# Attention and two expert layers in one kernel: the planner counts more columns per matmul, and all remainders go to VectorE

## The chip, the cores and the metric

One core of a Trainium2 chip runs the whole program. The metric is the device time of one execution in microseconds. The engines are named as in the profile: PE (TensorE matmul), PEld (its weight load), DVE (VectorE), ACT (ScalarE), POOL (GpSimd), SP (SyncE, here the queue that issues most transfers).

## What is computed

The reference chains three layers; the part that matters here is the second and third.

```
x = attention(q, k, v, f)                      # 2304 tokens of 512 numbers
e = argmax of the router's logits per token    # 8 experts
x[e == i] = gate * (relu(x[e == i] @ w1[i]) @ w2[i])      # w1: 512x1024, w2: 1024x512
x = maximum(maximum(x @ m1, x @ m2), x @ m3) @ m_out      # 512x768 three times, 768x512
```

All is float32. Each product is made of three matmuls of split operands: the high part of a number is a rounded copy, the low part ("remainder") is the number minus that copy; high times high, high times low and low times high are summed (`mm3`, L905 to L908).

## The kernel before, in words

Attention runs first (to about 216 us of the span), then the tokens are sorted by expert, and `moe` (from L911) computes both expert layers. Its order is not written out by hand: every step is a task with an engine (or a choice of two), a cost in microseconds, a priority (a due time `now`), dependences, and a slot of a buffer pool that it takes or frees. `Sched.run` (L184) picks, again and again, the task that can start first by its own count of time, and among those that can start at the same moment the one with the smallest priority; it then issues that task's instructions. So the costs and due times fix the order of the instructions in each engine's queue; at run time each engine works its queue strictly in that order and semaphores do the waiting.

The expert stage loops over k = 0 to 7, the experts in order of size, with room for C = 384, 352, ... 256 tokens (`CAP`). For each:

- `ph` (L906 to L908): 8 hidden tiles f, 12 matmuls each of C columns, from the tokens `x0`, `x1` (high, low) and the weight pieces `w_1_k_q`, q = 0 to 3;
- `h` (L1135 on ACT, L1141 on DVE): relu, high part and remainder of a hidden tile;
- `py`: 16 steps (q, d) of 6 matmuls, from `h` and `w_2_k_q`, then a copy into Y;
- `expert_piece` (L955): a weight piece is loaded into one of 3 `stg` buffers (L964), its high part is copied (L934, mostly ACT) into one of 4 `ring` buffers, and its remainder is taken (L951), on DVE or POOL;
- `tokens` (L1054): three gathers of the next expert's tokens by POOL (`gat`, L1065, 3 buffers), each transposed on PE (`xt`, L1072) into one of the two `ps_o` PSUM buffers, and split there by ACT (L934) and DVE (L1083) into `x0`, `x1`. So `xt1_0`, `xt1_1`, `xt1_2` are the three transposes that expert 1's first `ph` needs, and `xt2_0` the first of expert 2.

Two side jobs run beside this. `side_work` (L880) computes gates and the table of output rows; its last part, `scatter_table` (L834), makes four rounds on DVE (`pi`, `rm`, `rq`, `ohp`, `cc`, `rr`: L841 to L853) that feed four rounds of five small matmuls `ctps` on PE (L859), and then copies the sum out (`T`, L863). `ctps` holds one of the same two `ps_o` buffers from the first round to that copy. Its priority is a fixed 30. `shared_piece` (L988) loads the third layer's weights, two halves a piece through one `std` buffer, decodes each half in five DVE operations (L1005 to L1020, tiles `dec` and `sd`), copies the high part (ACT) and takes the remainder `m` (L1030, DVE or POOL).

The third layer then runs in six chunks of 384 tokens: 18 products `pm` of 12 matmuls, maxima on DVE (`tm`, L1240), high part and remainder `g` (L1251), and three output products `po` (L1266 to L1268). The tokens of a chunk are split from Y by L1199.

Priorities come from these lines (the cost of a matmul group in `now` is its columns over 2400):

```
gap = 24 * C / 2400
...
xdone[k + 1] = tokens(k + 1, now + 4 * gap, h_pe, [sorted_])
```

and in `tokens` the transposes get the priority `use - 6`.

Of the kernel before, what the change touches and what calls it, by code (L numbers as in the profile page):

```python
# [37 lines left out]
MC = 384  # L38
# [872 lines left out]
def moe(tc, g, x_dram, w1, w2, m2, mo, out, rp, es):  # L911
# [15 lines left out]
    sd.bias = {"DVE": 1.0, "Pool": 0.3}  # L927
    act = lambda n: 0.06 + n / 1200
    dve = lambda n: 0.15 + n / 960
    ENG = {"ACT": nc.scalar, "DVE": nc.vector, "Pool": nc.gpsimd}  # L930

    def copy(e, out, in_):
# [17 lines left out]
    def low(e, w, t):  # L950
        ENG[e].tensor_tensor(out=w[:, 1], in0=t, in1=w[:, 0].bitcast(F32), op=ALU.subtract)  # L951

    weight, wsplit, ahead = {}, {}, {}

    def expert_piece(n, k, q, use, deps=(), eng="SP"):  # L955
        src = (w1, w2)[n - 1]
        key = n, k, q
        raw = {}

        def load(e):  # L960
            dq = nc.sync if eng == "SP" else nc.scalar
            t = raw[0] = stg.tile([128, 1024], F32, tag="stg", name=f"stg_{n}_{k}_{q}")
            r = reg(dq, "expi" if k else "expi0", k, E - 1)
            dq.dma_start(out=t, in_=src[bass.ds(r, 1), q].rearrange("o p c -> (o p) c"))  # L964

        def hi(e):
            weight[key] = ring.tile([128, 2, 1024], F32R, tag="ring", name=f"w_{n}_{k}_{q}")
            high(e, weight[key], raw[0])

        ld = sd.task(eng, 1.5 if eng == "SP" else 0.1, load, use - 8, list(deps) + [ahead.get("stg")], get=("stg", key), lat=2.0 if eng == "SP" else 3.5)  # L970
        th = sd.task(("ACT", "DVE"), (0.95, 0.67), hi, use - 3, [ld, ahead.get("ring")], get=("ring", key))
        ahead["stg"], ahead["ring"] = ld, th
        tl = sd.task(("DVE", "Pool"), (1.13, 2.3), lambda e: low(e, weight[key], raw[0]), use - 3, [th], rel=[("stg", key)])
        wsplit[key] = tl
        return ld, th

    def bits(raw, q, v, n):
        r = raw.rearrange("p (n w) -> p n w", w=2)[:, 256 * q:256 * q + 256]
        lo, hi = r[:, :, 0], r[:, :, 1]
        t = scr.tile([128, 256], I32, tag="dect", name=f"dt{n}", bufs=1)  # L980
        u = scr.tile([128, 256], I32, tag="decu", name=f"du{n}", bufs=1)
        nc.vector.tensor_scalar(out=t, in0=hi, scalar1=3, scalar2=0x3FFFFFF8, op0=ALU.logical_shift_left, op1=ALU.bitwise_and)
        nc.vector.tensor_scalar(out=u, in0=hi, scalar1=0x7FFFFFFF, scalar2=None, op0=ALU.bitwise_and)
        nc.vector.scalar_tensor_tensor(out=t, in0=hi, scalar=-0x40000000, in1=t, op0=ALU.bitwise_and, op1=ALU.bitwise_or)
        nc.vector.scalar_tensor_tensor(out=t, in0=lo, scalar=29, in1=t, op0=ALU.logical_shift_right, op1=ALU.bitwise_or)
        nc.vector.scalar_tensor_tensor(out=v, in0=u, scalar=float(897 << 20), in1=t.bitcast(F32), op0=ALU.is_ge, op1=ALU.mult)

    def shared_piece(key, early, use, deps):  # L988
        w, j = key
# [3 lines left out]
        for h in range(2):  # L993
# [48 lines left out]
                         get=("ring", key) if new else None)  # L1042
            if new:
                ahead["ring"] = th
            lows.append(sd.task(("DVE", "Pool"), (dve(512), 1.3), lo, use - 3, [th], rel=[(pool_, (key, h))]))
        wsplit[key] = lows
        return lows[-1]

# [55 lines left out]

    zero = [sd.task("ACT", 1.8, lambda e, d=d: clear(e, d), now + 16, [wsplit[1, 0, 3]]) for d in range(KC)]
    mkeys = [(w, j) for j in range(3) for w in range(3)] + [("o", j) for j in range(3)]
    total = now + sum(CAP) * 192 / 2400
    shared = [wsplit[1, 0, 3]]
    for i, key in enumerate(mkeys[:M2EARLY]):
        shared.append(shared_piece(key, True, now + 30 + (total - now - 34) * (i + 1) / M2EARLY, [shared[max(0, i - 1)]]))  # L1110
# [2 lines left out]
    hlast, yev_last = [], []  # L1113
    for k in range(E):
        C = CAP[k]
        gap = 24 * C / 2400
        h_lo, h_pe, base = [], [], now
        for f in range(FC):
            q = f // 2
            t0 = now  # L1120
            key = 1, k, q

            def hmm(e, f=f, q=q, k=k, C=C):
                w = weight[1, k, q].rearrange("p s (k f) -> p s k f", k=KC)
                ph = hh["p", k, f] = ps_h.tile([128, 512], F32, tag="y", name=f"ph{k}_{f}")
                fs = slice(128 * (f % 2), 128 * (f % 2) + 128)
                for kc in range(KC):
                    mm3(nc, ph[:, 0:C], w[:, 0, kc, fs], w[:, 1, kc, fs], X[k][0][:, kc, 0:C], X[k][1][:, kc, 0:C],
                        kc == 0, kc == KC - 1)

            def relu(e, f=f, k=k, C=C):
                ht = hh[k, f] = hp.tile([128, 2, PADW], F32R, tag=f"h{f}", name=f"h{k}_{f}")
                ph = hh["p", k, f]
                if e == "ACT":
                    nc.scalar.activation(out=ht[:, 0, 0:C], in_=ph[:, 0:C], func=AF.Relu)  # L1135
                else:
                    nc.vector.tensor_scalar(out=ht[:, 0, 0:C], in0=ph[:, 0:C], scalar1=0.0, scalar2=None, op0=ALU.max)

            def rest(e, f=f, k=k, C=C):
                ht, ph = hh[k, f], hh["p", k, f]  # L1140
                nc.vector.scalar_tensor_tensor(out=ht[:, 1, 0:C], in0=ph[:, 0:C], scalar=0.0,  # L1141
                                               in1=ht[:, 0, 0:C].bitcast(F32), op0=ALU.max, op1=ALU.subtract)

            pe_ = sd.task("PE", 12 * C / 2400, hmm, t0, [wsplit[key]] + xdone[k] + yall, get=("y", ("h", k, f)),
                          rel=[("ring", key)] if f % 2 else [])
            now += 12 * C / 2400
            rl = sd.task(("ACT", "DVE"), (act(C), dve(C)), relu, now + 1, [pe_] + yprev[q])
            h_lo.append(sd.task("DVE", dve(C), rest, now + 1, [rl], rel=[("y", ("h", k, f))]))
            h_pe.append(pe_)
        for q in range(4):  # L1150
            expert_piece(2, k, q, now + q * gap, [sorted_] if k else [])
        if k + 1 < E:
            for q in range(4):
                expert_piece(1, k + 1, q, now + 4 * gap + q * 24 * CAP[k + 1] / 2400, [sorted_])
            xdone[k + 1] = tokens(k + 1, now + 4 * gap, h_pe, [sorted_])
        order = [(q, d) for q in range(4) for d in range(KC)] if k + 1 < E else [(q, d) for d in range(KC) for q in range(4)]
        last, pieces = {}, {q: [] for q in range(4)}
        for i, (q, d) in enumerate(order):
            def ymm(e, q=q, d=d, k=k, C=C):
                if q == 0:  # L1160
                    hh["y", k, d] = ps_y.tile([128, 512], F32, tag="y", name=f"py{k}_{d}")
                py = hh["y", k, d]
                w = weight[2, k, q].rearrange("p s (f d) -> p s f d", f=2)
                for f in range(2):
                    fc = 2 * q + f
                    ds_ = slice(128 * d, 128 * d + 128)
                    mm3(nc, py[:, 0:C], w[:, 0, f, ds_], w[:, 1, f, ds_], hh[k, fc][:, 0, 0:C], hh[k, fc][:, 1, 0:C],
                        fc == 0, fc == FC - 1)

            end = not any(q2 == q for q2, _ in order[i + 1:])  # L1170
            last[d] = sd.task("PE", 6 * C / 2400, ymm, now, [wsplit[2, k, q], h_lo[2 * q], h_lo[2 * q + 1], last.get(d)],
                              get=("y", ("y", k, d)) if q == 0 else None, rel=[("ring", (2, k, q))] if end else [])
            pieces[q].append(last[d])
            now += 6 * C / 2400
            if q == 3:
                def yev(e, d=d, k=k, C=C):
                    o = Y[d][:, bass.ds(reg(ENG[e], "offi", k, YW - C), C)] if k else Y[d][:, 0:C]
                    copy(e, o, hh["y", k, d][:, 0:C])

                prev = [ydone[-1][d], zero[d]] if ydone else []  # L1180
                t = sd.task(("ACT", "DVE"), (act(C), dve(C)), yev, now, [last[d]] + prev + [sorted_], rel=[("y", ("y", k, d))])
                yev_last.append(t)
# [7 lines left out]
    def ysplit(c, use, before):  # L1190
        done = []
        for kc in range(KC):
# [7 lines left out]
                                     in1=X["y", c][0][:, kc, :].bitcast(F32), op=ALU.subtract)  # L1200

            th = sd.task(("ACT", "DVE"), (act(MC), dve(MC) / 2), hi, use - 4, [ydone[-1][kc]] + before)
            done.append(sd.task(("DVE", "Pool"), (dve(MC), 1.0), lo, use - 4, [th]))
        return done

    before, oprev = hlast, [[] for _ in range(F2C)]
# [2 lines left out]
    for c in range(nchunk):  # L1209
        ys = ysplit(c, now, before)  # L1210
        before, glo = [], []
        for j in range(3):
            for f in range(2):
# [3 lines left out]
                for w in range(3):  # L1217
                    steps = [(kc, kc + 1) for kc in range(KC)] if c == 0 and fc == 0 else [(0, KC)]
                    for k0, k1 in steps:
                        def pmm(e, j=j, f=f, w=w, k0=k0, k1=k1, mx=mx, c=c):  # L1220
# [5 lines left out]
                            for kc in range(k0, k1):  # L1226
                                mm3(nc, ph[:, 0:MC], wm[:, 0, kc, fs], wm[:, 1, kc, fs], yh[:, kc, :], yl[:, kc, :],
                                    kc == 0, kc == KC - 1)

                        pe_ = sd.task("PE", 3 * (k1 - k0) * MC / 2400, pmm, now, wsplit[w, j] + (ys[k0:k1] if c == 0 and fc == 0 else ys) + yall,  # L1230
                                      get=("y", ("m", c, fc, w)) if k0 == 0 else None)
                        before.append(pe_)
                        now += 3 * (k1 - k0) * MC / 2400

                    def comb(e, w=w, mx=mx, c=c, fc=fc):
                        if w == 0:
# [14 lines left out]
                    ENG[e].tensor_tensor(out=ht[:, 1, :], in0=mx[0], in1=ht[:, 0, :].bitcast(F32), op=ALU.subtract)  # L1251

                th = sd.task(("ACT", "DVE"), (act(MC), dve(MC) / 2), ghi, now + 1, [prev] + oprev[fc])
                glo.append(sd.task(("DVE", "Pool"), (dve(MC), 1.0), glo_, now + 1, [th], rel=[("scr", ("m", c, fc))]))
        outs = []
        for b in range(m2c):
            col = c * m2c + b
# [17 lines left out]
                nc.gpsimd.indirect_dma_start(out=out, out_offset=bass.IndirectOffsetOnAxis(ap=g.sidx[:, col:col + 1], axis=0),  # L1275
                                             in_=o[1], in_offset=None, bounds_check=N - 1, oob_is_err=False)

            pe_ = sd.task("PE", 18 * DM / 2400, pout, now, glo + [x for j in range(3) for x in wsplit["o", j]], get=("y", ("o", col)))
            now += 18 * DM / 2400
            outs.append(pe_)  # L1280
            te = sd.task("ACT", act(DM), oev, now, [pe_], get=("scr", ("o", col)), rel=[("y", ("o", col))])
            sd.task("Pool", 1.04, put, now, [te], lat=3.0, rel=[("scr", ("o", col))])
# [177 lines left out]
```

## Time and profile before

| | |
|---|---|
| median of 3 runs | 780.75 us (780.52 to 781.61) |
| the profiled execution | 778.65 us, of which the span of the trace is 776.8 us |
| PE busy | 736.6 us, 95% of the span |
| PEld, DVE, ACT, POOL busy | 681.6, 443.4, 369.3, 237.5 us |
| mean granted clock of PE | 0.984 |

A time of the trace counts from the span's first instruction. Matmuls overlap in the pipeline, so the pace of PE is read from the distance between starts, and a wait from the bracket behind a row, which gives the idle time before it and what ended it.

### The profile page before, as it was taken

How to read it: one execution, taken by the hardware profiler on the slowest of the kernel's cores; microseconds unless marked ns; L12 is line 12 of the kernel's file. 1: busy time of each engine (PE TensorE's matmuls, PEld its weight loads, DVE VectorE, ACT ScalarE, POOL GpSimd, SP SyncE). 2: the span in 40 equal slices, each digit the busy share in tenths (PEclk: the TensorE clock that was granted, in tenths of full speed). 3: DMA queues.
4: the chain of work that ended last, by engine and by line, in shares of the span. 5: the costliest groups of instructions: out<-in, count | busy, mean ns of one | idle time of the engine just before them, and what ended most of it. 6: DMA issues, size and time to landing. Idle time of an engine off the chain costs nothing.

```text
span 776.8 us, 13376 instructions
## 1 busy us (share of the span) xinstructions
PE 736.6 (95%) x4862; PEld 681.6 (88%) x4862; DVE 443.4 (57%) x1075; ACT 369.3 (48%) x871; POOL 237.5 (31%) x189
## 2 busy tenths in 40 slices
PE   2999999999949998999999999999999999999996
PEld 1887888878739988999999999989999899999995
DVE  6877877868478997868677878931301212112110
ACT  5778988989548344455454553231211212112111
POOL 7456452550030534234231104331221212212112
PEclk9999999999959999999999999999999999999998
DMA  9787877751155545565555562210000000100001
GB/s 223 199 203 182 213 168 190 165 118 23 32 182 183 193 146 197 185 215 202 175 207 185 208 221 93 82 42 1 1 41 1 28 14 1 41 0 17 25 1 43
DMA packets 44614, 90.19 MB, mean 116 GB/s; under 512 B 23320, under 2 KB 23320, under 8 KB 44544
## 3 DMA queue, kind: packets, MB, share of 16 engines
q1 hardware_dynamic: 40960, 77.83, 34.1%
q0 software_dynamic: 3152, 9.88, 3.5%
q10 hardware_dynamic: 432, 1.57, 0.5%
q8 instruction: 40, 0.66, 0.3%
q14 instruction: 30, 0.25, 0.1%
HBM read 74.97 MB, written 9.44 MB: 109 GB/s over the span
## 4 chain that ended last, share of the span: by engine, by line
PE 84%; DVE 7%; DMA 4%; ACT 2%; issue 2%; POOL 0%; SPq 0%; POOLq 0%; DVEq 0%; ACTq 0%
PE pm L907 10%; PE pm L908 10%; PE pm L906 10%; PE s L344 8%; PE po L459 6%; PE t L397 5%; PE ph L908 4%; PE ph L907 4%; PE ph L906 4%; PE py L906 3%; PE py L908 3%; PE py L907 3%; PE po L1268 3%; PE po L1267 3%; PE po L1266 3%; PE pb L478 2%
## 5 line engine op out<-in xcount | busy, mean ns | idle before, releaser
L1240 DVE TENSOR_TENSOR tm<-pm,tm 128x384 f32<-128x384 f32 x72 | 40.1, 556 | 199.4 <-PE pm L908 198.2
L907 PE MATMUL pm<-x_y,m 128*128 128x384 f32 x432 | 144.6, 335 | 0.0
L908 PE MATMUL pm<-x_y,m 128*128 128x384 f32 x432 | 144.5, 334 | 0.0
L906 PE MATMUL pm<-x_y,m 128*128 128x384 f32 x432 | 144.5, 334 | 0.0
L381 ACT ACTIVATE P<-P,nm 128x576 f32<-128x576 f32 (+4 forms) x160 | 88.2, 554 | 7.0 <-DVE nm L361 6.9
L934 ACT ACTIVATE w<-stg 128x1024 fp32r<-128x1024 f32 x63 | 66.2, 1056 | 37.1 <-DMA stg<-in_w_dram 17.8
L951 DVE TENSOR_TENSOR w<-stg,w 128x1024 fp32r<-128x1024 f32 x54 | 69.9, 1299 | 22.3 <-ACT w L934 21.7
L907 PE MATMUL ph<-x,w 128*128 128x384 f32 (+7 forms) x256 | 79.9, 312 | 2.6 <-DVE x L1083 2.6
L907 PEld LDWEIGHTS pm<-x_y,m 128*128 128x128 f32 x432 | 81.1, 188 | 0.6 <-POOL x_y L1199 0.3
L906 PEld LDWEIGHTS pm<-x_y,m 128*128 128x128 f32 x432 | 81.1, 188 | 0.2
L908 PEld LDWEIGHTS pm<-x_y,m 128*128 128x128 f32 x432 | 81.1, 188 | 0.0
L906 PE MATMUL py<-h,w 128*128 128x384 f32 (+7 forms) x256 | 79.6, 311 | 1.3 <-DVE h L1141 1.3
L906 PE MATMUL ph<-x,w 128*128 128x384 f32 (+7 forms) x256 | 80.0, 313 | 0.7 <-ACT x L934 0.7
L908 PE MATMUL ph<-x,w 128*128 128x384 f32 (+7 forms) x256 | 79.9, 312 | 0.7 <-DVE w L951 0.7
L344 PE MATMUL s<-R,At 128*128 128x192 f32 (+1 forms) x192 | 70.1, 374 | 11.1 <-DVE At L271 10.8
L1251 POOL TENSOR_TENSOR g<-tm,g 128x384 fp32r<-128x384 f32 x34 | 36.5, 1073 | 141.4 <-ACT g L934 141.4
L908 PE MATMUL py<-h,w 128*128 128x384 f32 (+7 forms) x256 | 78.5, 307 | 0.4 <-DVE w L951 0.4
L907 PE MATMUL py<-h,w 128*128 128x384 f32 (+7 forms) x256 | 78.3, 306 | 0.0
L934 ACT ACTIVATE g<-tm 128x384 fp32r<-128x384 f32 x36 | 18.8, 523 | 115.9 <-DVE tm L1240 115.9
L361 DVE CUSTOM_DVE_ANT_0 P<-s,mask 128x288 f32<-128x288 f32 (+4 forms) x160 | 64.7, 422 | 15.3 <-PE s L344 11.4
L324 POOL TENSOR_TENSOR R<-k,R 64x1152 fp32r<-64x1152 f32 x15 | 39.6, 2638 | 77.3 <-PE s L344 23.1
L344 PE MATMUL s<-R,Bt 66*128 66x192 f32 (+1 forms) x192 | 59.0, 315 | 4.4 <-DMA Bt<-At 4.4
(246 smaller groups left out, 1602.5 us busy)
## 6 DMA issues: line engine op xcount, KB each, us to landing
stg<-in_w_dram SPq DMA_DIRECT2D x61, 512.0 KB
q<-in_q_dram SPq DMA_DIRECT2D x32, 288.0 KB
k<-in_k_dram SPq DMA_DIRECT2D x32, 288.0 KB
sd<-in_m_dram SPq DMA_DIRECT2D x18, 512.0 KB
Bt<-At SPq DMA_DIRECT2D x16, 288.0 KB
v<-in_v_dram SPq DMA_DIRECT2D x4, 1024.0 KB
x_dram<-XL SPq DMA_DIRECT2D x64, 64.0 KB
sd_o<-in_mo_dram SPq DMA_DIRECT2D x6, 512.0 KB
```

Of the source, the lines that this page charges most:

```text
L324: nc.gpsimd.tensor_tensor(out=R2[i][0:64], in0=raws[p][1][0:64], in1=R1[i][0:64].bitcast(F32), op=ALU.subtract)
L344: nc.tensor.matmul(st[:, 0:wp], lt[0:kk, r, ROW0[t]:ROW0[t] + 128], rt[0:kk, r, j0:j0 + wp], start=(ps_i == 0), stop=(ps_i == 1))
L361: nc.vector.tensor_tensor_reduce(out=P[0:n, j0:j0 + w], in0=st_.pop((h, t, k))[0:n, 0:w], in1=g.mask[0:n, m0:m0 + w], scale=-0.125, scalar ...
L381: nc.scalar.activation(out=P[0:n, 0:ext], in_=P[0:n, 0:ext], func=AF.Exp, bias=nm[0:n, k:k + 1], scale=-1.0, accum_out=sums[b][0:n, t, h % ...
L397: nc.tensor.transpose(w[:, 128 * a:128 * a + 128], P[:, 128 * a:128 * a + 128], g.ident)
L459: nc.tensor.matmul(po[64 * r:64 * r + 64, lo - c0:w], vt[b][0:n, a, (2 * hp + r) * D:(2 * hp + r + 1) * D], PT[(2 * p + r) % NPT][0:n, a, ...
L906: nc.tensor.matmul(out, whi, xhi, start=start, stop=False)
L907: nc.tensor.matmul(out, whi, xlo, start=False, stop=False)
L908: nc.tensor.matmul(out, wlo, xhi, start=False, stop=stop)
L934: nc.scalar.activation(out=out, in_=in_, func=AF.Copy)
L951: ENG[e].tensor_tensor(out=w[:, 1], in0=t, in1=w[:, 0].bitcast(F32), op=ALU.subtract)
L1240: nc.vector.tensor_tensor(out=mx[0], in0=mx["p", w][:, 0:MC], in1=mx[0], op=ALU.max)
```

## The change

The planner's cost of a matmul of n columns becomes (n + 31)/2400 us instead of n/2400, in the costs and in the due times alike. And the four kinds of remainder in `moe` that could go to DVE or POOL (L951, L1030, L1199, L1251) can go to DVE alone. `bits`, which nothing calls, is removed; lines behind it move up by ten.

```diff
+    mms = lambda count, n: count * (n + 31) / 2400
...
-        tl = sd.task(("DVE", "Pool"), (1.13, 2.3), lambda e: low(e, weight[key], raw[0]), use - 3, [th], rel=[("stg", key)])
+        tl = sd.task("DVE", 1.13, lambda e: low(e, weight[key], raw[0]), use - 3, [th], rel=[("stg", key)])
...
-            lows.append(sd.task(("DVE", "Pool"), (dve(512), 1.3), lo, use - 3, [th], rel=[(pool_, (key, h))]))
+            lows.append(sd.task("DVE", dve(512), lo, use - 3, [th], rel=[(pool_, (key, h))]))
...
-    total = now + sum(CAP) * 192 / 2400
+    total = now + sum(mms(192, n) for n in CAP)
...
-        gap = 24 * C / 2400
+        gap = mms(24, C)
...
-            pe_ = sd.task("PE", 12 * C / 2400, hmm, t0, [wsplit[key]] + xdone[k] + yall, get=("y", ("h", k, f)),
+            pe_ = sd.task("PE", mms(12, C), hmm, t0, [wsplit[key]] + xdone[k] + yall, get=("y", ("h", k, f)),
                           rel=[("ring", key)] if f % 2 else [])
-            now += 12 * C / 2400
+            now += mms(12, C)
...
-            done.append(sd.task(("DVE", "Pool"), (dve(MC), 1.0), lo, use - 4, [th]))
+            done.append(sd.task("DVE", dve(MC), lo, use - 4, [th]))
...
-                glo.append(sd.task(("DVE", "Pool"), (dve(MC), 1.0), glo_, now + 1, [th], rel=[("scr", ("m", c, fc))]))
+                glo.append(sd.task("DVE", dve(MC), glo_, now + 1, [th], rel=[("scr", ("m", c, fc))]))
```

The same replacement stands at every other place that adds PE time to `now` or to a task's cost.

What this does to the queues shows at three places. First PE, between expert 0's second product (`py0`) and expert 1's first (`ph1_0`). Before:

```order
L1072 MATMUL xt1_0_3837<-ident_78,gat1_0_3545 128x128 x4
L1072 MATMUL xt1_1_3843<-ident_78,gat1_1_3549 128x128 x4
...
L906 MATMUL py0_3_3752<-h0_5_3687,w_2_0_2_3762 128x384
...
L859 MATMUL ctps_3885<-rr_3814,ohp_3803 128x90
...
L1072 MATMUL xt1_2_3892<-ident_78,gat1_2_3568 128x96 x4
...
L906 MATMUL py0_3_3752<-h0_7_3750,w_2_0_3_3795 128x384
...
L906 MATMUL ph1_0_3945<-x0_1_3849,w_1_1_0_3835 128x352
...
L859 MATMUL ctps_3885<-rr_3937,ohp_3922 128x90
```

and after the change:

```order
L859 MATMUL ctps_3838<-rr_3802,ohp_3791 128x90
...
L1062 MATMUL xt1_0_3862<-ident_78,gat1_0_3545 128x128 x4
...
L906 MATMUL py0_3_3764<-h0_7_3746,w_2_0_3_3789 128x384
...
L859 MATMUL ctps_3838<-rr_3891,ohp_3867 128x90
...
L859 MATMUL ctps_3838<-rr_3945,ohp_3940 128x90
...
L859 MATMUL ctps_3838<-rr_3975,ohp_3968 128x90
...
L1062 MATMUL xt1_1_3992<-ident_78,gat1_1_3549 128x128 x4
L1062 MATMUL xt1_2_3999<-ident_78,gat1_2_3568 128x96 x4
L1062 MATMUL xt2_0_4014<-ident_78,gat2_0_3877 128x128 x4
L906 MATMUL ph1_0_4023<-x0_1_3879,w_1_1_0_3821 128x352
```

The first `ctps` round now stands ahead of `xt1_0` (the transposes' due time grew, the table's priority of 30 did not), so the table takes a `ps_o` buffer first; `xt1_1` is the next to want it and stands, with `xt1_2`, behind all four rounds. Before, one round stood ahead of `ph1_0`.

Second DVE, from the last remainder of expert 0's hidden tiles (`h0_7`) to the last split of expert 1's tokens, after the change. Each `pi` opens a round of the table, the first L1005 row a half of the third layer's weights:

```order
L1131 SCALAR_TENSOR_TENSOR h0_7_3746<-ph0_7_3702,h0_7_3746 128x384
L841 CAST pi_3758<-offt_3697 128x5
...
L952 TENSOR_TENSOR w_2_0_3_3789<-stg_2_0_3_3730,w_2_0_3_3789 128x1024
...
L1073 TENSOR_TENSOR x1_1_3880<-xt1_0_3862,x0_1_3879 128x4x128
...
L863 COPY T_3985<-ctps_3838 128x90
...
L1073 TENSOR_TENSOR x1_1_3880<-xt1_1_3992,x0_1_3879 128x4x128
L1073 TENSOR_TENSOR x1_1_3880<-xt1_2_3999,x0_1_3879 128x4x96
```

Between the first and the last of these stand four rounds of the table, six weight remainders (`w_2_0_2`, `w_2_0_3`, `w_1_1_0` to `w_1_1_3`), both halves of the first shared piece with their remainders `m`, and the split of `xt1_0`. Before, the split of `xt1_2` had two rounds and one half ahead of it, and `T` came after expert 1's `h1_7`.

Third POOL, in the same stretch. Before:

```order
L1065 DMA gat1_2_3568<-x_dram_65,gidx_3465 96x512
L951 TENSOR_TENSOR w_2_0_3_3795<-stg_2_0_3_3744,w_2_0_3_3795 128x1024
L1065 DMA gat2_0_3852<-x_dram_65,gidx_3465 128x512
L1065 DMA gat2_1_3864<-x_dram_65,gidx_3465 128x512
L1030 TENSOR_TENSOR m_0_0_3862<-sd_0_0_0_3640,m_0_0_3862 128x512
L1065 DMA gat2_2_3907<-x_dram_65,gidx_3465 80x512
L951 TENSOR_TENSOR w_1_1_2_3932<-stg_1_1_2_3881,w_1_1_2_3932 128x1024
```

and after:

```order
L1055 DMA gat1_2_3568<-x_dram_65,gidx_3465 96x512
L1055 DMA gat2_0_3877<-x_dram_65,gidx_3465 128x512
L1055 DMA gat2_1_4005<-x_dram_65,gidx_3465 128x512
L1055 DMA gat2_2_4011<-x_dram_65,gidx_3465 80x512
L1055 DMA gat3_0_4021<-x_dram_65,gidx_3465 128x512
```

POOL keeps its gathers and loses all its tensor operations of `moe`, 74 in number: 10 of L951, 22 of L1030, 8 of L1199 and 34 of L1251.

## Rows read from the trace of the kernel before

**Rows 1.** Stretches: length; busy PE, PEld, DVE, ACT, POOL; clock; DMA share; GB/s.

```profile
266.00:304.00 38.00, 33.87 (x223) 32.49 (x221) 34.52 (x53) 15.83 (x25) 17.10 (x9) 1.00 0.56 199
...
306.00:308.00 2.00, 2.00 (x9) 2.00 (x8) 0.96 (x1) 1.43 (x3) 1.09 (x1) 0.50 0.00 0
...
510.00:560.00 50.00, 50.00 (x272) 47.66 (x271) 10.35 (x17) 10.55 (x21) 11.16 (x11) 1.00 0.04 17
```

**Rows 2.** Waits of PE: line waited for, us in total, times, longest.

```profile
PE ph L907 <- DVE x L1083: 2.6, 2, 2.1
PE py L906 <- DVE h L1141: 1.3, 1, 1.3
PE ph L908 <- DVE w L951: 0.7, 1, 0.7
...
PE py L908 <- DVE w L951: 0.4, 1, 0.4
```

**Rows 3.** Timeline of PE: start, us, instruction, idle before it and releaser.

```profile
266.02 0.32 PE L906 MATMUL ph<-x,w 128*128 128x352 f32 x1
...
278.97 0.37 PE L859 MATMUL ctps<-rr,ohp 128*128 128x90 f16 x5 [0.28 <-DVE rr L853]
```

**Rows 4.** Timeline of DVE, 250 to 300 us.

```profile
250.77 0.16 DVE L841 CAST pi<-offt 128x5 int32<-128x5 f32 x1
...
251.25 1.23 DVE L951 TENSOR_TENSOR w<-stg,w 128x1024 fp32r<-128x1024 f32 x1
252.39 3.03 DVE L724 TENSOR_TENSOR ohp<-iota,rm 128x640 f16<-128x640 f32 x1
...
256.45 0.42 DVE L1005 TENSOR_SCALAR dec<-sd 128x512 int32<-128x512 int32 x1
...
259.30 1.22 DVE L951 TENSOR_TENSOR w<-stg,w 128x1024 fp32r<-128x1024 f32 x1
260.44 1.28 DVE L1083 TENSOR_TENSOR x<-xt,x 128x512 fp32r<-128x512 f32 x2
...
284.54 0.16 DVE L841 CAST pi<-offt 128x5 int32<-128x5 f32 x1
...
286.86 0.95 DVE L1141 SCALAR_TENSOR_TENSOR h<-ph,h 128x352 fp32r<-128x352 f32 x2
...
293.05 0.24 DVE L863 COPY T<-ctps 128x90 f32<-128x90 f32 x1
...
294.05 0.68 DVE L1030 TENSOR_TENSOR m<-sd,m 128x512 fp32r<-128x512 f32 x1
...
298.85 3.23 DVE L1005 TENSOR_SCALAR dec<-sd 128x512 int32<-128x512 int32 x1 [1.62 <-DMA sd<-in_m_dram]
```

**Rows 5.** Groups of POOL by form: count, busy us, mean ns; idle before them.

```profile
L951 POOL TENSOR_TENSOR w<-stg,w 128x1024 fp32r<-128x1024 f32 x10 | 25.6, 2557 | 63.1 <-ACT w L934 40.6 <-PE py L908 22.5
```

**Rows 6.** Timeline of POOL.

```profile
252.25 2.49 POOL L951 TENSOR_TENSOR w<-stg,w 128x1024 fp32r<-128x1024 f32 x1 [22.52 <-PE py L908]
...
298.44 0.92 POOL L1065 DMA_INDIRECT gat<-x_dram,gidx  x1 [0.30 <-issue]
299.38 2.41 POOL L951 TENSOR_TENSOR w<-stg,w 128x1024 fp32r<-128x1024 f32 x1
```

**Rows 7.** Timelines of PE, ACT, DVE: one token transpose and its split, expert 0.

```profile
224.90 1.09 PE L1072 MATMUL xt<-ident,gat 128*128 128x128 f32 x4 [0.24 <-DMA gat<-x_dram,gidx]
...
226.02 0.60 ACT L934 ACTIVATE x<-xt 128x512 fp32r<-128x512 f32 x1 [0.73 <-PE xt L1072]
...
226.65 0.69 DVE L1083 TENSOR_TENSOR x<-xt,x 128x512 fp32r<-128x512 f32 x1 [0.64 <-ACT x L934]
```

**Rows 8.** Timeline of PE, start of expert 2's first product.

```profile
303.99 0.42 PE L907 MATMUL ph<-x,w 128*128 128x336 f32 x1 [2.14 <-DVE x L1083]
...
308.09 0.31 PE L908 MATMUL ph<-x,w 128*128 128x336 f32 x1
...
309.93 0.32 PE L908 MATMUL ph<-x,w 128*128 128x336 f32 x1
```

More of the change, by code (lines that the diff above doesn't have):

```diff
@@ L972, in expert_piece @@
         ahead["stg"], ahead["ring"] = ld, th
-        tl = sd.task(("DVE", "Pool"), (1.13, 2.3), lambda e: low(e, weight[key], raw[0]), use - 3, [th], rel=[("stg", key)])
+        tl = sd.task("DVE", 1.13, lambda e: low(e, weight[key], raw[0]), use - 3, [th], rel=[("stg", key)])
         wsplit[key] = tl
         return ld, th
[L977 to L986, printed above, removed]
     def shared_piece(key, early, use, deps):
@@ L1153, in moe @@
             for q in range(4):
-                expert_piece(1, k + 1, q, now + 4 * gap + q * 24 * CAP[k + 1] / 2400, [sorted_])
+                expert_piece(1, k + 1, q, now + 4 * gap + q * mms(24, CAP[k + 1]), [sorted_])
             xdone[k + 1] = tokens(k + 1, now + 4 * gap, h_pe, [sorted_])
@@ L1170, in moe @@
             end = not any(q2 == q for q2, _ in order[i + 1:])
-            last[d] = sd.task("PE", 6 * C / 2400, ymm, now, [wsplit[2, k, q], h_lo[2 * q], h_lo[2 * q + 1], last.get(d)],
+            last[d] = sd.task("PE", mms(6, C), ymm, now, [wsplit[2, k, q], h_lo[2 * q], h_lo[2 * q + 1], last.get(d)],
                               get=("y", ("y", k, d)) if q == 0 else None, rel=[("ring", (2, k, q))] if end else [])
             pieces[q].append(last[d])
-            now += 6 * C / 2400
+            now += mms(6, C)
             if q == 3:
@@ L1228, in pmm @@
                                     kc == 0, kc == KC - 1)
-                        pe_ = sd.task("PE", 3 * (k1 - k0) * MC / 2400, pmm, now, wsplit[w, j] + (ys[k0:k1] if c == 0 and fc == 0 else ys) + yall,
+                        pe_ = sd.task("PE", mms(3 * (k1 - k0), MC), pmm, now, wsplit[w, j] + (ys[k0:k1] if c == 0 and fc == 0 else ys) + yall,
                                       get=("y", ("m", c, fc, w)) if k0 == 0 else None)
                         before.append(pe_)
-                        now += 3 * (k1 - k0) * MC / 2400
+                        now += mms(3 * (k1 - k0), MC)
                     def comb(e, w=w, mx=mx, c=c, fc=fc):
@@ L1276, in put @@
                                              in_=o[1], in_offset=None, bounds_check=N - 1, oob_is_err=False)
-            pe_ = sd.task("PE", 18 * DM / 2400, pout, now, glo + [x for j in range(3) for x in wsplit["o", j]], get=("y", ("o", col)))
-            now += 18 * DM / 2400
+            pe_ = sd.task("PE", mms(18, DM), pout, now, glo + [x for j in range(3) for x in wsplit["o", j]], get=("y", ("o", col)))
+            now += mms(18, DM)
             outs.append(pe_)
```

## The prediction

> **What bounds the kernel now.** I read the table of stretches first [rows 1]. In the third layer PE is busy for the whole of its stretch (50.00 of 50 us) and all else is mostly idle: there nothing but PE's own work counts. In the expert stage PE is nearly always busy too, but not in expert 1: 33.87 of 38 us from 266 to 304. DVE is the next engine there, 34.52 us busy, and POOL has 17.10. So I read PE's waits next [rows 2]: all that this change can take from PE in the expert stage is in these few rows, and each ends on DVE, on the splits of tokens (2.6 us), on a hidden tile (1.3), on weight remainders (0.7 and 0.4); the timeline adds 0.28 for a round of the table [rows 3]. Last I read DVE's timeline around them [rows 4]. Two operations stick out: `ohp` with 3.03 us and a decode step with 3.23, where the same step takes 0.42 at 256.45. Both stand beside a POOL remainder of about 2.4 us (252.25 and 299.38) [rows 6] and end 0.3 to 0.7 us after it. So POOL's tensor operations hold DVE up: POOL needs 2.56 us for a weight remainder on average [rows 5], DVE 1.22 [rows 4], and in the meantime some DVE operation can lose as long.
>
> **The change part by part.**
>
> *The remainders of the third layer.* 34 of L1251 and a few of L1199 pass from POOL to DVE. DVE has 39 of 50 us free and PE waits for nothing [rows 1], so I cost this at 0. A last product of a chunk needs the last `g`, but only in the last 3 of its 18 matmuls; those before it cover the remainder on either engine. If that cover were gone, the price would be below one us a chunk. The kernel's last transfers follow the last PE product as before.
>
> *The remainders of the expert stage.* 10 of L951 at 1.22 us and most of 22 of L1030 at 0.68 [rows 4] are about 25 us more for DVE. Against it stand the blocked operations: `ohp` lost about 2.2 us and the decode step 2.8 [rows 4]. In 266 to 304, where four weight remainders ran on POOL whole, DVE would do them and an `m` in 5.6 us, so two such losses pay for them. I take DVE's load as not greater than before, and the waits that such losses caused as gone.
>
> *The order around expert 1, which sets the forecast.* PE's queue now has all four rounds of `ctps`, then `xt1_1`, `xt1_2` and `xt2_0`, ahead of `ph1_0`. PE works in order, so `ph1_0` cannot start before DVE has done all four rounds and the copy `T`. What stands on DVE from the first `pi` to `T`, with distances between starts of clear rows [rows 4]: four rounds at 2.32 (284.54 to 286.86) are 9.28; six weight remainders at 1.14 (251.25 to 252.39) 6.84; two decodes at 2.85 (256.45 to 259.30) 5.70; one split 0.64; two `m` 1.36; `T` 0.24. Sum 24.06 us. The chain starts at 250.77, where ACT's last hidden tile of expert 0 puts it before and after alike, so `T` ends at 274.83. I find no longer wait inside: PE ends `py0` at about 266 as before [rows 3], the weight pieces' ring buffers come free as `py0` goes on, and the second half of the shared piece, loaded once the first `m` is done, has 4.6 us of other DVE work to arrive in.
>
> From `T` on: `xt1_1` on PE 1.09 us, its copy on ACT 0.60, its split on DVE 0.69 with hops of 0.03 [rows 7], 277.3; `xt2_0` needs the `ps_o` buffer that this split frees, 1.09 more: `ph1_0` starts at **278.4 instead of 266.02** [rows 3], **+12.4 us**. I take the transposes at the slow pace of those rows, since PE has little to do for 10 us.
>
> *The clock.* After the wait of 2.14 us at 303.99 the granted clock is 0.50 from 306 to 308 [rows 1, 8], the 1.2 GHz level. The 16 matmuls from 303.99 to 308.09 took 4.10 us, the 12 from 308.09 to 309.93 took 1.84, or 0.153 each; so the slow ones cost 4.10 - 16 x 0.153 = **+1.65 us**. A longer wait will bring the same once.
>
> *Work that lies inside the wait.* Three rounds of `ctps` (at most 0.37 each [rows 3]) and `xt2_0` (about 0.55 at full clock, half of 1.09) leave the time behind `ph1_0`: between 0.6 and 1.65, I take **-1.2 us**.
>
> *Old waits.* Of expert 1 and 2: 0.42 (the rest of the 2.6 after the 2.14 at 303.99 [rows 2, 8]), 0.28, 1.30, 2.14 and the slow clock after the last, 1.65: 5.8 us. All come from late splits, the table's rounds or DVE operations beside POOL; the table is done, POOL is quiet, and PE is busy for 33.87 us in expert 1 [rows 1] while DVE's work for one expert is 8 x 1.14 for weights, 8 x 0.48 for hidden tiles, 3 x 0.64 for splits and 2 x 3.53 for two halves with their `m` [rows 4], 22 us. I take **-5.8**, with 0 as the other bound. Of the late ones, 0.7 and 0.4 [rows 2], which hang on transfers of weights too, I take half: **-0.6**.
>
> Sum: 12.4 + 1.65 - 1.2 - 5.8 - 0.6 = **+6.45 us**. The profiled execution would be 778.65 + 6.45 = 785.1 (span 776.8 + 6.45 = 783.2). The median of the runs shown, 780.75, is 2.1 above the profiled one, so the same on top of it gives **787.2 us**.
>
> One rule of the Trainium skill would lengthen the list on DVE. The row first: the decode step at 298.85 would have ended at 299.27, before the POOL remainder at 299.38 began, and yet it ended after that [rows 4, 6]; a gather's issue ran from 298.44 to 299.36 [rows 6]. The Trainium skill, "SBUF — State Buffer", section on the practical consequences of the shared port pair, says that a DVE operation in a two-port mode and GpSimd's writing of descriptors block each other, whoever starts first holding the other for its whole length; the trace agrees with that. By it one gather (`gat2_0`) in the list would add up to 0.9 us, an estimate, and the sum would be +7.4.
>
> **The rivals.** About 0.2%, 1.6 us, is what a measurement of this kernel can tell from no change.
>
> *DVE becomes the bound* (chance 0.12). DVE takes 74 operations more, experts 1 and 2 wait for it as before and the late waits stay. For it: DVE is 34.52 of 38 us busy there [rows 1]. Against it: the blocked operations. It decides from the point where DVE has more than some 34 us of work in expert 1. Time: 12.4 + 1.65 - 1.2 = +12.85, 793.6 us. Beside it stands the Trainium skill, "Perfetto Trace Analysis", section "Optimizing Scalar/DVE Operations": with a saturated DVE it may make sense to offload even to GPSIMD, which speaks against this change; in the same breath it warns that the two share a port and that it might not help. No run here shows DVE with these operations yet.
>
> *The wait comes short* (chance 0.11, within 0.2%). If `T` ended some 5 to 6 us earlier, old and new waits would balance: 780.8 us. It needs the list of 24.06 to run in about 18, though its rows are clear ones already, or to start that much earlier, though its rounds wait for `offt`, which is done only just before 250.77.
>
> *Faster* (chance 0.07). The new wait does not form, since the table's rounds find gaps on DVE before PE ends `py0` at 266; then `T` would have to come by about 265, 10 us sooner than the rows give. PE would keep only the gains: 780.75 - 5.8 - 0.6 = 774.4 us. For it: with POOL quiet, DVE is faster than in any row beside a POOL remainder. Against it: the sum was made of clear rows already.
>
> **How the numbers follow.** My forecast has the chance 0.70. The likeliest time is 787.2 us. For the range: if all old waits go and the list is 2 us shorter, about +3.5; if the wait is nearly balanced, +1.6; at the other end none of the old waits goes, +12.85. I give 782.4 to 793.6; outside lie the faster case, most of the balanced one and the tail of the first rival. Slower by over 0.2%: 0.70 + 0.12 = 0.82; within 0.2%: 0.11; faster: 0.07.
>
> **What would show each step.** In PE's waits: one of about 6 us before the third or fourth `ctps` round and several of a few tenths to 3 us between the rounds, the transposes and `ph1_0`, 10 us or more together, with `ph1_0` near 278.4 of the span. In the clock: 0.50 around 275 to 282, and 1.00 around 306. In the rows of DVE: no operation of L724 or L1005 above 1.5 us, L951 64 times at 1.22, and POOL with gathers and output transfers alone. In the third layer: PE busy 50.00 of 50 as now. Wrong it would be if `ph1_0` started before 273, if PE waited more than 2 us in experts 2 to 7, or if the third layer's chunks changed their length of 50 us.

## The result, and the profile after

The change made the kernel slower: 783.14 us (median of 13 runs, 781.84 to 787.34) against 778.80 for the kernel before (13 runs, 776.00 to 781.61). The ratio is 1.0067, 95% interval 1.0053 to 1.0081, which is +5.2 us (4.1 to 6.3) on 778.80; the medians alone differ by 4.3. The profiled execution took 784.80 us, its span 783.0.

The page of the changed kernel (busy time of the engines; the clock in 40 slices; the weight remainders). Behind `bits` the line numbers are ten lower than before, from L930 up to it one higher:

```profile
PE 738.2 (94%) x4862; PEld 684.8 (87%) x4862; DVE 450.3 (58%) x1149; ACT 370.9 (47%) x871; POOL 134.1 (17%) x115
...
PEclk9999999999969979999999999999999999999999
...
L952 DVE TENSOR_TENSOR w<-stg,w 128x1024 fp32r<-128x1024 f32 x64 | 78.1, 1222 | 28.1 <-ACT w L935 27.6
```

POOL lost 103 us of work (it was busy 237.5) and DVE took 74 operations more, yet DVE is busy only 6.9 us longer (450.3 against 443.4). All 64 weight remainders are on DVE. A new dip of the clock stands in the 15th slice.

Waits of PE from 225 to 480 us, columns as in [rows 2]:

```profile
PE ctps L859 <- DVE rr L853: 8.0, 2, 6.0
PE xt L1062 <- DMA gat<-x_dram,gidx: 4.2, 2, 4.0
PE xt L1062 <- DVE ov L781: 1.6, 1, 1.6
PE xt L1062 <- DVE x L1073: 0.8, 1, 0.8
PE ph L906 <- ACT x L935: 0.7, 1, 0.7
```

All four groups of [rows 2] are gone; the second, third and last line here belong to the start of expert 0, before and after alike. New are the first and the fourth, both at expert 1. Timeline of PE there, columns as in [rows 3]:

```profile
268.53 0.38 PE L859 MATMUL ctps<-rr,ohp 128*128 128x90 f16 x5
270.94 0.37 PE L859 MATMUL ctps<-rr,ohp 128*128 128x90 f16 x5 [2.03 <-DVE rr L853]
277.26 0.54 PE L859 MATMUL ctps<-rr,ohp 128*128 128x90 f16 x5 [5.95 <-DVE rr L853]
277.59 1.73 PE L1062 MATMUL xt<-ident,gat 128*128 128x128 f32 x8
280.09 1.11 PE L1062 MATMUL xt<-ident,gat 128*128 128x128 f32 x4 [0.77 <-DVE x L1073]
280.86 0.64 PE L906 MATMUL ph<-x,w 128*128 128x352 f32 x1
...
284.43 0.32 PE L906 MATMUL ph<-x,w 128*128 128x352 f32 x1
```

Rounds three and four of the table are waited for, round two (268.53) is not; only then come the transposes and, at 280.86, `ph1_0`. The 12 matmuls from there to 284.43 took 3.57 us; 12 at the later pace of 0.16 take 1.92. DVE in the same time (the chain from the first `pi` to the copy `T`; compare [rows 4]):

```profile
253.25 0.16 DVE L841 CAST pi<-offt 128x5 int32<-128x5 f32 x1
...
254.86 0.82 DVE L724 TENSOR_TENSOR ohp<-iota,rm 128x640 f16<-128x640 f32 x1
...
263.62 0.63 DVE L853 TENSOR_TENSOR rr<-cc,val 128x450 f16<-128x450 f16 x1
264.16 0.69 DVE L1073 TENSOR_TENSOR x<-xt,x 128x512 fp32r<-128x512 f32 x1
...
267.08 1.23 DVE L952 TENSOR_TENSOR w<-stg,w 128x1024 fp32r<-128x1024 f32 x1 [0.50 <-ACT w L935]
...
268.95 0.82 DVE L724 TENSOR_TENSOR ohp<-iota,rm 128x640 f16<-128x640 f32 x1 [0.28 <-PE ctps L859]
...
277.83 0.25 DVE L863 COPY T<-ctps 128x90 f32<-128x90 f32 x1
```

`ohp` needs 0.82 us where it took 3.03 beside POOL. The chain has only two gaps, 0.50 and 0.28. Stretches, columns as in [rows 1]:

```profile
266.00:304.00 38.00, 29.25 (x177) 28.70 (x176) 30.03 (x60) 15.27 (x25) 3.02 (x3) 0.87 0.52 176
...
276.00:278.00 2.00, 0.74 (x7) 0.84 (x8) 1.91 (x6) 0.00 (x0) 0.00 (x0) 0.50 0.00 0
282.00:284.00 2.00, 2.00 (x9) 2.00 (x8) 1.93 (x4) 0.00 (x0) 0.63 (x1) 0.50 0.62 160
...
306.00:308.00 2.00, 2.00 (x16) 1.98 (x15) 1.66 (x2) 1.56 (x2) 0.00 (x0) 1.00 0.73 256
510.00:560.00 50.00, 50.00 (x274) 47.85 (x273) 14.08 (x27) 10.91 (x21) 3.02 (x3) 1.00 0.04 16
```

PE lost 4.62 us in the first stretch (33.87 before). The slow clock moved from 306 to expert 1, and the third layer is filled by PE as before.

Where the time went is read best from the starts of PE's stages. The table gives the start of the first matmul of `ph0`, and of the others the time since then (from the timelines of PE; `pm` is the third layer's first product, "end" PE's last):

| | before | before, 2nd trace | change | rem_only | cols_only | early25 | late36 | late42 |
|---|---|---|---|---|---|---|---|---|
| `ph0` at | 229.20 | 229.48 | 232.16 | 228.67 | 229.24 | 229.43 | 229.82 | 229.43 |
| `ph1` | 36.82 | 36.93 | 48.70 | 36.66 | 59.09 | 52.97 | 37.64 | 36.98 |
| `ph2` | 72.34 | 72.16 | 82.02 | 69.49 | 92.92 | 85.70 | 72.39 | 69.91 |
| `py2` | 91.01 | 88.83 | 96.75 | 84.21 | 107.64 | 100.42 | 87.12 | 84.63 |
| `ph6` | 191.43 | 189.26 | 197.15 | 185.92 | 215.62 | 201.43 | 187.53 | 185.72 |
| `pm` | 241.40 | 238.91 | 245.12 | 235.95 | 264.97 | 251.57 | 235.50 | 233.69 |
| end | 540.48 | 537.99 | 543.74 | 535.63 | 563.80 | 550.69 | 534.13 | 532.32 |

Behind `ph0` the change costs 3.26 us against the one trace of before and 5.75 against the other. By stage, against the first: +11.88 up to `ph1`, -6.14 from there to `py2`, about 0 to `ph6`, -2.5 behind it.

### The profile page after: what moved, and what is told of

The parts are those of the page before. It is cut to its first block, busy times and chain, and to the rows that moved or that the text cites. A ratio compares the mean times of both kernels' runs of the same rounds, so it can differ in the third digit from the quotient of the medians.

```text
span 783.0 us, 13295 instructions
## 1 busy us (share of the span) xinstructions
PE 738.2 (94%) x4862; PEld 684.8 (87%) x4862; DVE 450.3 (58%) x1149; ACT 370.9 (47%) x871; POOL 134.1 (17%) x115
## 5 line engine op out<-in xcount | busy, mean ns | idle before, releaser
L952 DVE TENSOR_TENSOR w<-stg,w 128x1024 fp32r<-128x1024 f32 x64 | 78.1, 1222 | 28.1 <-ACT w L935 27.6
L1265 POOL DMA_INDIRECT out_dram<-oo,ctidx x18 | 17.7, 984 | 334.4 <-ACT oo L1262 331.4
L1055 POOL DMA_INDIRECT gat<-x_dram,gidx x23 | 25.0, 1086 | 222.5 <-PE xt L1062 173.7
```

The costliest lines, as they stand in the source:

```text
L1055: nc.gpsimd.indirect_dma_start(out=t[0:n], out_offset=None, in_=x_dram, in_offset=bass.IndirectOffsetOnAxis(ap=idx, axis=0))
```

## The experiments

Theory A: the price is the order alone, since all rounds of the table stand ahead of `ph1_0`; a quiet POOL is a gain. Theory B: DVE with the added remainders is the bound.

**rem_only**: the remainders on DVE, the columns counted as before.

```diff
-    mms = lambda count, n: count * (n + 31) / 2400
+    mms = lambda count, n: count * n / 2400
```

> All remainders on VectorE, the planner's old cost of n/2400 kept; PE's order around expert 1 is that of the kernel before (xt1_0 and xt1_1 ahead of the table's first round, one round ahead of ph1_0). Theory A (the new order at expert 1 costs about 12 us and a cold start of 1.65, quiet GpSimd gives back the old waits): no long wait, expert 1 and 2 lose their waits, from the start of expert 0's first product to the end some 5 to 8 us less than the 547.6 of before, ratio to before about 0.990 to 0.994. Theory B (VectorE is the bound once it takes 74 operations more): waits on VectorE in experts 1 to 3 as before or longer, ratio 1.000 to 1.010.

Measured: 774.51 us, ratio 0.9950 (0.9932 to 0.9968). Waits of PE, 225 to 480 us:

```profile
PE ph L908 <- DVE w L952: 1.0, 2, 0.7
PE py L908 <- DVE w L952: 1.0, 3, 0.6
```

By itself the part that loads DVE more is a gain. B falls. The ratio is just above A's figure, and from `ph0` to the end of the span it is 4.9 us less (542.7 against 547.6), just under the 5 to 8 expected: the late waits for weight remainders stay and there are five of them, where before had two (0.41 and 0.74).

**cols_only**: 31 columns more; the four remainders may go to POOL again.

```diff
-        tl = sd.task("DVE", 1.13, lambda e: low(e, weight[key], raw[0]), use - 3, [th], rel=[("stg", key)])
+        tl = sd.task(("DVE", "Pool"), (1.13, 2.3), lambda e: low(e, weight[key], raw[0]), use - 3, [th], rel=[("stg", key)])
```

and so at the three other places.

> The planner counts 31 columns more, the remainders may go to GpSimd as before; PE's order around expert 1 is that of the change (all four rounds of the table ahead of ph1_0). Theory A: a wait of 10 us or more before ph1_0, some GpSimd remainders still block VectorE inside the list, so ph1_0 starts 48.7 us after expert 0's first product or up to 4 us later, and part of the old waits stays: ratio to before 1.007 to 1.016, above that of the change. Theory B: without the added VectorE work the kernel is as fast as before or faster, ratio 1.000 or less.

Measured: 799.52 us, ratio 1.0259 (1.0233 to 1.0285). The direction is A's, the size is not: `ph1` starts 59.09 us after `ph0`. PE's queue at this place has the order of the change; the difference is DVE's list beside POOL. Timeline of DVE, then of POOL:

```profile
252.72 3.02 DVE L724 TENSOR_TENSOR ohp<-iota,rm 128x640 f16<-128x640 f32 x1
255.67 0.24 DVE L847 TENSOR_TENSOR cc<-io,rq 128x90 f16<-128x90 f32 x1
...
263.09 2.60 DVE L847 TENSOR_TENSOR cc<-io,rq 128x90 f16<-128x90 f32 x1
...
270.57 2.39 DVE L847 TENSOR_TENSOR cc<-io,rq 128x90 f16<-128x90 f32 x1
```

```profile
252.58 2.48 POOL L952 TENSOR_TENSOR w<-stg,w 128x1024 fp32r<-128x1024 f32 x1 [22.82 <-ACT w L935]
...
263.16 2.41 POOL L952 TENSOR_TENSOR w<-stg,w 128x1024 fp32r<-128x1024 f32 x1
270.22 2.63 POOL L952 TENSOR_TENSOR w<-stg,w 128x1024 fp32r<-128x1024 f32 x1 [4.65 <-ACT w L935]
```

The same `cc` that takes 0.24 us alone takes 2.60 and 2.39, and ends just behind a remainder on POOL (265.69 behind 265.57). From `pi` to the end of `T` DVE needs 33.86 us (251.11 to 284.97), 9.0 more than in the change. Of that, 8.9 are lost beside POOL (five rows above their clear length: 2.20, 2.36 and 2.15 here, 1.10 for a `cc` at 276.71, 1.11 for a `pi` at 260.77), 5.7 are a third decode and its wait for the load, which end ahead of `T` here:

```profile
281.86 0.43 DVE L995 TENSOR_SCALAR dec<-sd 128x512 int32<-128x512 int32 x1 [2.87 <-DMA sd<-in_m_dram]
```

and three weight remainders and two `m` that POOL takes over save 3 x 1.14 + 2 x 0.68 = 4.8; the change's two gaps, 0.78, are not there. The expectation had allowed too little for what POOL costs DVE. PE in the same trace, and one later wait:

```profile
279.38 1.09 PE L1062 MATMUL xt<-ident,gat 128*128 128x128 f32 x4
285.03 0.90 PE L1062 MATMUL xt<-ident,gat 96*128 96x96 f32 x4 [4.56 <-DVE T L863]
...
382.94 0.66 PE L1062 MATMUL xt<-ident,gat 48*128 48x48 f32 x4 [3.29 <-DVE x L1073]
```

`xt1_1` runs at 279.38, right behind the fourth round; `xt1_2` alone waits for `T`. Against this run the other edit of the change is a gain of 16 us, and not at expert 1 alone: from `ph0` on, 10.4 us of the difference between the two traces stand ahead of `ph1` and 9.7 behind it. The largest part behind it is the wait at 382.94 with a granted clock of 0.50 from 384 to 388: from expert 3's second product to expert 4's first it is 21.32 us here and 15.53 in the change. There DVE had itself waited 3.55 us for a load of the third layer's weights, ahead of the split; so not all of the 16 us is POOL holding DVE up.

**early25**: the kernel before with the side work's priority 25 in place of 30, nothing else. PE's order at expert 1 becomes almost that of the change.

```diff
-    sd.chain(side_work(nc, g, g.cp, rp, ps_o), 30.0, [sorted_])
+    sd.chain(side_work(nc, g, g.cp, rp, ps_o), 25.0, [sorted_])
```

> The kernel before with nothing changed but the side work's priority, 30 to 25: TensorE's order at expert 1 becomes almost that of the change (table rounds and xt2_0 ahead of expert 1's first product), while the columns counted and GpSimd's remainders stay as before. Theory A (the order alone brings the wait): expert 1's first product 55 to 62 us behind expert 0's (59.09 with 31 columns and GpSimd's remainders, 36.82 before), waits on TensorE for the table of 15 us or more, the clock at 0.50 behind them, time 1.015 to 1.035 of the kernel before. Theory B (the wait comes from VectorE's added remainders or from the 31 columns elsewhere): 37 to 40 us, time within 0.5% of the kernel before.

Measured: 789.08 us in its one run, 1.0145 of 777.83. Waits of PE:

```profile
PE ctps L859 <- DVE rr L853: 11.5, 2, 6.3
```

The wait is there with neither of the two edits, so the order alone brings it. It is smaller than I wrote (52.97, not 55 or more; 11.5 us, not 15; a ratio just under 1.015). DVE, then POOL:

```profile
252.20 2.45 DVE L847 TENSOR_TENSOR cc<-io,rq 128x90 f16<-128x90 f32 x1
...
260.79 4.38 DVE L718 TENSOR_SCALAR rq<-pi 128x5 int32<-128x5 int32 x1
265.08 0.81 DVE L724 TENSOR_TENSOR ohp<-iota,rm 128x640 f16<-128x640 f32 x1
```

```profile
259.44 2.00 POOL L1065 DMA_INDIRECT gat<-x_dram,gidx  x1 [4.91 <-PE ctps L859]
261.46 1.33 POOL L1030 TENSOR_TENSOR m<-sd,m 128x512 fp32r<-128x512 f32 x1
262.74 2.39 POOL L951 TENSOR_TENSOR w<-stg,w 128x1024 fp32r<-128x1024 f32 x1
```

An operation on five numbers a partition, 0.16 us elsewhere, stood for 4.38 us and ended at 265.17, behind the last of three POOL instructions in a row (265.13). At its usual length it would have ended at 260.95, when only the gather was running.

**late36**: the change, with the side work's priority 36 in place of 30, so that most of the table stands behind `ph1_0` again.

```diff
-    sd.chain(side_work(nc, g, g.cp, rp, ps_o), 30.0, [sorted_])
+    sd.chain(side_work(nc, g, g.cp, rp, ps_o), 36.0, [sorted_])
```

> The change with the priority of the table's side work at 36 instead of 30, nothing else: xt1_0, xt1_1 and xt1_2 stand ahead of the table's first round again, one round stands ahead of ph1_0. Theory A: ph1_0 starts about 37 us after expert 0's first product instead of 48.7, no cold start, and the savings of the change stay: 10 to 13 us less than the change, ratio to before about 0.990. Theory B: VectorE's list is only moved, PE waits for it in expert 1 or 2 instead; no more than 4 us less than the change.

Measured: 772.76 us, ratio 0.9924 (0.9904 to 0.9944); `ph1` 37.64 us after `ph0`. With both edits kept, the one number gives back 10 us. A holds; it beats both kernels. One wait is left at experts 1 and 2:

```profile
PE ph L907 <- DVE x L1073: 1.7, 1, 1.7
```

**late42**: the same with priority 42; as with 36, one round stands ahead of `ph1_0` and three behind.

```diff
-    sd.chain(side_work(nc, g, g.cp, rp, ps_o), 30.0, [sorted_])
+    sd.chain(side_work(nc, g, g.cp, rp, ps_o), 42.0, [sorted_])
```

> Theory A (the price is the order at expert 1: the table of capacities stands ahead of expert 1's first product): with the side work's priority at 42 all rounds of the table but one stand behind expert 1's first product on TensorE, so there is no wait of over 2 us before it; its first product about 37 us behind expert 0's (37.64 at priority 36, 48.70 in the change), no stretch at granted clock 0.50 around it, time 0.990 to 0.994 of the kernel before, within 0.2% of the version at priority 36. Its one wait of 1.65 us for the copy of x there should go or stay under 2 us. Theory B (VectorE, which now makes all remainders, is the bound): the time stays near the change's 783 us, 1.003 or more.

Measured: 771.49 us, ratio 0.9919 (0.9891 to 0.9948). Waits of PE, 225 to 480 us:

```profile
PE xt L1062 <- DMA gat<-x_dram,gidx: 1.8, 2, 1.3
PE ph L906 <- ACT x L935: 0.7, 1, 0.7
PE xt L1062 <- DVE dec L999: 0.6, 1, 0.6
```

The first two lines are the start of expert 0, the third one transpose of expert 3; no wait at expert 1 or 2 is left. It is the fastest version found; from late36 the intervals do not part it.

**after_again** and **before_again**: both kernels unchanged, for a second trace.

> The changed kernel once more, for a second trace: in the first one expert 0's first product started at 232.16 us against 229.20 in the trace of before, though attention's queues are the same. If that is chance between executions, the start falls anywhere between 228 and 233 and the stretch behind it stays within 0.5 us of 550.8. If the change slows attention, the start is again near 232.

> The kernel before, unchanged, for a second trace. If the 2.96 us by which the change's expert stage began later are chance of an execution, expert 0's first product starts between 228.5 and 232.5 us and every start behind it, measured from there, stands within 0.1 us of the first trace (36.82 for expert 1, 72.34 for expert 2, 540.48 for the end). If they belong to the change, it starts at 229.20 within 0.1 us again.

Measured: the change 782.69 us, `ph0` at 230.11, all behind it within 0.13 us of the first trace. So of the 2.96 us by which its expert stage began later, 2.05 are chance of an execution. It still is later than all the others (228.67 to 229.82, the last with both edits in it); whether a few tenths belong to the change is open. The kernel before: 776.43 us, `ph0` at 229.48, but not all within 0.1 us: `py2` comes 2.18 earlier. One wait on PE, and the stretch behind it:

```profile
303.62 0.42 PE L907 MATMUL ph<-x,w 128*128 128x336 f32 x1 [1.68 <-DVE x L1083]
```

```profile
306.00:308.00 2.00, 2.00 (x15) 2.00 (x14) 1.34 (x2) 1.50 (x4) 0.72 (x1) 1.00 0.07 27
```

The wait is 1.68 us, not 2.14 [rows 8], and no slow clock follows it [rows 1 has 0.50 at the same place].

## Why the prediction was right, and which terms were off

The forecast was right: slower, by the mechanism named, inside the range, though the median lies only 0.7 us above the range's lower end. 787.2 stood 4.1 us above the median. Half of that is the base: three runs gave 780.75, thirteen gave 778.80. The other half is in the sum.

*The new wait: +12.4 forecast, +11.88 measured.* The list on DVE was summed to 24.06 us and took 24.83 (253.25 to 278.08). "I find no longer wait inside" was wrong by the two gaps, 0.78; the rows themselves were priced to a few hundredths. The step behind the list was read wrongly, ahead of the prediction too: `xt1_1` does not wait for `T`'s `ps_o` buffer. Its row starts at 277.59, right behind the fourth round, and `T` ends at 278.08; in cols_only it starts 5.35 us before `T` does. So the last `m` and `T` (277.12 to 278.08) were not on PE's path here, and from `T` to `ph1_0` it took 2.78, not 3.57. The chain began 21.09 us after `ph0`, not 21.57. The first and second of these differences cancel (+0.77, -0.79), so that the sum came within 0.5 us is partly luck. The waits in PE's list are 8.8 us together, where "10 us or more" was to show the step; by the rows from 268.53 to 280.09 most of the rest is PE's own work that now stands ahead of `ph1_0`, three rounds and `xt2_0`, and transposes at the slow clock. That this order is the cause, early25 and late36 show: it brings the wait without either edit, and without it both edits bring no wait for the table.

*The clock: +1.65 forecast, 3.57 - 1.92 = 1.65 measured,* and 0.50 stands where it was said.

*Work inside the wait and old waits: -1.2 - 5.8 + 1.65 = -5.35 forecast from `ph1` to `py2`, -6.14 measured.* All four waits went. But two of the terms are not the same in every execution: the second trace of the kernel before has a wait of 1.68 where the first has 2.14, and no slow clock behind it, and against that the same stretch gave -3.85 (51.90 to 48.05 us). Which of the two is the rule stays open. The mean granted clock of the whole run is 0.984, as in the first trace, in 15 of the 19 runs of the kernel before that were timed beside the experiments, and 0.986 to 0.988 in the other four (0.988 in the second trace). That speaks for the slow clock as the usual case, but it does not show where in those runs the clock was low. A single profile cannot tell a wait that is always there from one at the edge; such a term wants a second trace before it is given one size.

*Late waits: -0.6 forecast, about -2.5 measured* (behind `ph6`: 349.05 us before, 348.73 in its second trace, 346.59 with the change). This is the mis-sized term. The two waits named, 0.41 and 0.74, went whole, not by half; 0.46 lies behind `pm`, and the rest, about 0.85, in distances too small for a row of their own. By these traces it comes from the 31 columns together with the quiet POOL: rem_only alone has 349.71 there, cols_only 348.18, the change, late36 and late42 346.6. So the edit of the planner was of use late in the stage; only at expert 1 it did harm.

*The remainders on DVE: costed as no greater load, and the trace goes further.* `ohp` is at 0.82, a decode step at 0.42 (257.84), 64 remainders at 1.22, as forecast. 74 operations at clear prices are 10 x 1.22 + 16 x 0.68 + 6 x 0.67 + 34 x 0.56 + 8 x 0.52, 50 us (the prices of the changed kernel's groups). The durations of all DVE rows, summed, rose by 10.9 (490.7 to 501.6); the busy time, which rose by 6.9, counts the overlap of two rows once. So some 39 us of DVE's durations before were hold-ups, an estimate that takes all its other work as alike. The first decode step is an example, before and after:

```profile
L1005 DVE TENSOR_SCALAR dec<-sd 128x512 int32<-128x512 int32 x18 | 14.1, 784 | 8.1 <-DMA sd<-in_m_dram 8.0
L995 DVE TENSOR_SCALAR dec<-sd 128x512 int32<-128x512 int32 x18 | 7.6, 424 | 10.3 <-DMA sd<-in_m_dram 10.3
```

The first rival (DVE becomes the bound) fell with rem_only, where the same load on DVE is a gain. The Trainium skill, "Perfetto Trace Analysis", section "Optimizing Scalar/DVE Operations", which was set beside that rival, also says that such an offload might not help; here its warning was the part that held: taking the offload back alone gave a ratio of 0.9950 (rem_only).

*The rule that would add 0.9.* One gather did run inside the list, at 263.75 for 1.32 us. The DVE rows beside it, `rr` 0.63 and `x` 0.69, are as long as elsewhere, so nothing was added. The Trainium skill, "SBUF — State Buffer", section "Who interferes with whom", gives `tensor_tensor` no two-port mode, though with both inputs in SBUF it contends with what GpSimd reads, and says that it did not stall transfers; both rows are such operations, and the trace agrees. I applied the rule without looking at which operations stand beside the gather: `rq` of early25, which stood behind one from 260.79 on, is a TENSOR_SCALAR.

## What to carry to other kernels

When a planner's costs change, look for the jobs whose priority is a fixed number: here the due times grew past a constant 30, a side job moved ahead of a product, and that product started 11.9 us later. Price an order by summing the list that the waiting engine must see done, from clear rows; that was good to 0.8 us of 25. And two edits that arrive as one should be timed apart: one alone was worth -0.5%, the other +2.6%, and both with a later side job -0.8%.

## What the runs showed of the hardware that was not expected

- A blocked DVE operation can wait for several POOL instructions in a row: 4.38 us for one of 0.16, over the end of a gather, a remainder of 1.33 and one of 2.39 (early25).
- 0.46 us of wait went with about 1.5 us more: in two traces of the same program the same matmul waited 2.14 us, with the granted clock at 0.50 behind it, and 1.68 us, with 1.00 behind it; from expert 2's first product to its second the two took 18.67 and 16.67 us.
- Up to the first product of the expert stage, two executions of the same program differed by 2.05 us.
